# Top-k attention and a gated projection on one core: the last weight piece of a slot goes to GpSimd, and the first pair of slots splits earlier

## The chip, the cores and the metric

One core of a Trainium2 chip. The metric is the time of one execution in microseconds (us), measured on the device. PE is TensorE, DVE VectorE, ACT ScalarE, POOL GpSimd and SP SyncE; SPq is SP's queue, which issues nearly all transfers.

## The reference

```python
def _attn_ref(q, k, v):                       # each 8 x 8 x 576 x 64
    scores = scale * np.matmul(q, k.transpose(0, 1, 3, 2))
    kth = np.partition(scores, -32, axis=-1)[..., -32:-31]
    scores = np.where(scores >= kth, scores, -1e9)
    attn = np.exp(scores - np.max(scores, axis=-1, keepdims=True))
    attn = attn / (np.sum(attn, axis=-1, keepdims=True) + 1e-09)
    return np.matmul(attn, v)

def _moe_ref(x, w_in, w_out):                 # x: 4608 x 512, made of the 8 heads
    h = x @ w_in                              # 512 x 2048
    g = h * (1.0 / (1.0 + np.exp(-1.702 * h)))
    return g @ w_out                          # 2048 x 512
```

`q`, `k` and `v` are 32-bit floats. The two weights come out of the set-up as 64-bit floats, so the kernel reads them as pairs of 32-bit words.

## The kernel before, in words

**Slots.** A batch has 8 heads in 4 pairs, and 576 queries: four tiles of 128 and a tail of 64. A slot is one pair of heads with one tile of queries (or the tails of two pairs), 128 queries of two heads at a time; 18 slots a batch, 144 in all. The order of all instructions is written out by hand: `opening()`, then `slot(n)` for n = 0 to 10 (`SETTLED`), `first_pair(11)`, then pairs of slots in `filling_pair` (from n = 13, `STEADY`) and `steady_pair`, and at the end what is left of the second product.

**A slot's way.** `scores` (PE, sixteen matmuls into four banks), `copy_scores` (ScalarE), `pair_up` (VectorE: larger and smaller of the two halves of the keys, which makes the first two rounds of the search half as wide), `topk` (VectorE: four rounds that find eight values each, three that remove them; 14 operations), `bounds` (GpSimd: the thirty-second and the largest value, scaled), `mask` and `exps` (ScalarE; `exps` sums as well), `invert` (VectorE; from slot 12 on its first half on GpSimd), and then two ways. In slots up to 9, `divide` makes two diagonal matrices of the inverse sums on GpSimd (`by`, a single buffer) and PE multiplies with them to turn the probabilities (`turn_main`, `turn_ends`), and ScalarE copies them out. From slot 10 on, `normalize` (GpSimd) scales the probabilities, `split` (ScalarE) sorts their half-words and SP's queue writes them to memory as `rows`, and `turn_by_dma` reads them back transposed. Last come `values` (PE) and the copy into `xT`. When the four pairs of a tile are done, `hidden` (first product, four chunks of 128 at a time), `tanh` (ScalarE), `gate` (VectorE or GpSimd) and `project` (second product) follow; the first two blocks are done whole, the later ones by seven products of quarters in place of eight. `leave` copies a finished block out on ScalarE; with `project(True)` that waits until `leave_all()`.

**Weights.** There are 32 pieces of 128x512 numbers: two for slot 0 and three each for slots 1 to 10 (`by_slot`). A piece is read into one of seven buffers (`raws`), in the slot before its own, as soon as the piece that lay there is finished, and made into a 32-bit float in five steps: `size` (ScalarE: magnitude of the high word, rebased), `shift` (VectorE: three bits up, which drops the sign bit), `low` (ScalarE: top bits of the low word), `put_sign` (GpSimd: the sign, as a 16-bit zero, into the upper half of the low word) and `add` (GpSimd). `slot(n)` does the sizes after the copy of the scores, the shifts behind the thirteenth of the search's 14 operations, the lows at the end, and the signs and additions in slot n + 1: three of these six before the diagonals, three behind them.

**Queues.** Each engine works in order. In slots 4 to 10, GpSimd's is: bounds, sign, addition, sign, two diagonals, addition, sign, addition. ScalarE's is: mask, exponentials, copy of the scores, tanh, three sizes, copies out of PE's turns, three lows (in slot 5 the tanh comes behind the lows).

**The opening.** `prepare_first` turns the first pair of heads, `scores(0)` and `pair_first` follow, then PE turns the second pair (`prepare`, of which `prepare_ends` is the tails), and `scores(1)`. `stay_warm(count)` is a number of matmuls whose result nobody reads.

**The first pair.** `first_pair(11)` handles slots 11 and 12: `find(m, at)` runs a search and puts `pair_up` behind its eighth operation and `invert(m - 1)` behind operation `at`.

Of the kernel before, what the change touches and what calls it, by code (L numbers as in the profile page):

```python
# [33 lines left out]
def kernel(  # L34
# [101 lines left out]
    def round_piece(n):  # L136

        c, g = pieces[n]
        dst = wout[:, g, :] if c is None else win[:, c, g * PIECE : (g + 1) * PIECE]
        both = raw.pop(n)  # L140
        words = both.rearrange("p (n w) -> p n w", w=2)
        low, high = words[:, :, 0], words[:, :, 1].bitcast(F32)
        parts = both.bitcast(U16).rearrange("p (n h) -> p n h", h=4)
        sign = parts[:, :, 1].bitcast(F16)
        bits, whole = dst.bitcast(U32), dst.bitcast(I32)

        def put_sign():
            nc.gpsimd.tensor_scalar(sign, high, TO_ZERO, 1.0, op0=ALU.mult, op1=ALU.mult)

        def add():  # L150
            nc.gpsimd.tensor_tensor(out=whole, in0=whole, in1=low.bitcast(I32), op=ALU.add)
            finished.append(None)

        return {
            "size": lambda: nc.scalar.activation(dst, high, AF.Abs, scale=REBASE),
            "shift": lambda: nc.vector.tensor_scalar(bits, bits, 3, None, op0=ALU.logical_shift_left),
            "low": lambda: nc.scalar.mul(out=low.bitcast(I32), in_=low, mul=2.0**-29),
            "finish": [put_sign, add],
        }
# [87 lines left out]
    def prepare(name, b, hp):  # L247
        prepare_main(name, b, hp)
        if name == "k":
            prepare_ends(b, hp)  # L250
# [98 lines left out]
    def pair_first():  # L349

        sc = st[0]["sc"] = scp.tile([P, 2, S], F32, name="sc")
        ranked[0] = rank.tile([P, 2, 2, HALF], F32, name="ranked")
        part = lambda i, c: (sc[:, i, c * HALF : (c + 1) * HALF], score_banks[:, i, c, 0:HALF])
        for i in range(2):
            nc.scalar.copy(out=part(i, 1)[0], in_=part(i, 1)[1])
            for c, op in enumerate((ALU.max, ALU.min)):
                nc.vector.tensor_tensor(out=ranked[0][:, i, c, :], in0=part(i, 0)[1], in1=part(i, 1)[0], op=op)
        for i in range(2):
            nc.scalar.copy(out=part(i, 0)[0], in_=part(i, 0)[1])

    def topk(n):

# [67 lines left out]
    def divide(n):  # L430

        invert(n)
        by = st[n]["by"] = diagonals[:]
        for i in range(2):
            nc.gpsimd.tensor_scalar(by[:, i, :], ident[:], st[n]["rden"][:, i : i + 1], 1.0, op0=ALU.mult, op1=ALU.mult)
# [412 lines left out]
    def finish_one():  # L848
        unfinished.pop(0)()
# [34 lines left out]
    def opening():  # L884

        stay_warm(8, v_tail[:, 0, :, :].rearrange("p j d -> p (j d)"))
        load("q", 0, 0, nc.sync)
        load("k", 0, 0, nc.scalar)
        for hp in range(2):
            for name in "qk":  # L890
                if hp:
                    load(name, 0, hp)
        for x in by_slot[0]:
            load_piece(x)
        prepare_first()
        scores(0)
        pair_first()
        stay_warm(2)
        for name in "qk":
            prepare(name, 0, 1)  # L900
        early.extend(round_piece(x) for x in by_slot[0])
        for piece in early:
            piece["size"]()
        scores(1)
        copy_scores(1)
        prepare_rest()
        for hp in range(2, NP):
            for name in "qk":
                load(name, 0, hp)
        load_v(0, 0)  # L910
        for x in by_slot[1]:
            load_piece(x)
# [11 lines left out]
    def slot(n):  # L924

        todo = later.pop(n, [])
        for fn, args in todo:
            if fn not in (prepare, prepare_by_dma, load_piece):
                fn(*args)
        preparing = [(fn, args) for fn, args in todo if fn is prepare or fn is prepare_by_dma]  # L930
        some = [round_piece(x) for x in by_slot.get(n, [])] if n else early
        steps = {name: [piece[name] for piece in some] for name in ("size", "shift", "low")}

        def do(name, count):
            for _ in range(min(count, len(steps[name]))):
                steps[name].pop(0)()

        if n == 0:
            steps["size"].clear()
            do("low", 3)  # L940
        else:
            exponentials(n - 1, bring_all if n % 4 == 1 and n > TURNS + 1 else lambda: None)
            if n == TURNS + 1:
                stay_warm(14)
                bring_all()
            copy_scores(n + 1)
            bring_all()
            if 1 < n <= TURNS:
                turn_main(n - 2)
                turn_ends(n - 2)  # L950
            if n > TURNS + 1:
                tanh(False)
            do("size", 3)
            if n == TURNS + 1:
                do("low", 3)
                tanh(False)
        for i, op in enumerate(topk(n)):
            op()
            if i == 1:
                for _ in range(min(3, len(unfinished))):  # L960
                    finish_one()
            if i == (9 if n < 3 else 7):
                if n > 0:
                    divide(n - 1)
                while unfinished:
                    finish_one()
                for fn, args in todo:
                    if fn is load_piece:
                        fn(*args)
            if i == 9:  # L970
                pair_up(n + 1)
            if i == 12:
                do("shift", 3)
            if i == (13 if n == TURNS + 1 else 10):
                gate()
        bounds(n)
        for piece in some:
            unfinished.extend(piece["finish"])
        if n < NP:
            for fn, args in preparing:  # L980
                fn(*args)
        if n >= TURNS:
            turn_main(n - 1)
            turn_ends(n - 1)
        do("low", 3)
        scores(n + 2)
        if n == SETTLED:
            copy_scores(n + 2)
        if n == 0:
            return  # L990
        idle = not ready and n < TURNS
        if 1 < n <= TURNS:
            values(n - 2, put_off if n == TURNS else None)
        if n >= TURNS:
            values(n - 1, put_off)
        if n >= NP:
            for fn, args in preparing:
                fn(*args)
        if n > PROJECTS and may_project(2):
            project(n == SETTLED)  # L1000
        if idle:
            stay_warm(8)
        hidden()
# [23 lines left out]
    def find(m, at):  # L1027

        for i, op in enumerate(topk(m) if live(m) else [lambda: None] * 14):
            op()  # L1030
            if i == 7 and live(m) and live(m + 1):
                pair_up(m + 1)
            if i == at and live(m - 1):
                invert(m - 1)
            if i > 1 and len(unfinished) > (2 if m == SETTLED + 1 else 0):
                finish_one()
# [5 lines left out]
    def first_pair(n):  # L1042

        begin, prepare_some = dues(n)
        gate()
        bring_all()
        exponentials(n - 1)
        find(n, 10)
        scores(n + 2)
        copy_scores(n + 2)  # L1050
        leave_all()
        tanh(True)
        prepare_some()
        some = [round_piece(x) for x in by_slot.get(n, [])]
        for piece in some:
            piece["size"]()
        hidden(ps_t)
        project_one()
        normalize(n - 1)
        tanh(True)  # L1060
        bounds(n)
        finish_one()
        finish_one()
        for piece in some:
            piece["shift"]()
            piece["low"]()
            unfinished.extend(piece["finish"])
        while unfinished:
            finish_one()
        split(n - 1)  # L1070
        begin(0)
        turn_by_dma(n - 1)
        exponentials(n, leave_all)
        find(n + 1, 10)
        project_one()
        scores(n + 3)
        copy_scores(n + 3)
        leave_all()
        normalize(n)
        split(n)  # L1080
        begin(1)
        turn_by_dma(n)
        bounds(n + 1)
        gate()
        summing.extend(weight_sums("t1", "b12", "b11") + weight_sums("t2", "b22", "t1") + weight_sums("t4", "b21", "t2"))
# [176 lines left out]
```

## Time and profile before

| | |
|---|---|
| median of 3 runs | 1389.51 us (1389.18 to 1391.13) |
| the profiled execution | 1392.55 us, of which its span 1390.8 us |
| TensorE clock granted over the span | 0.987 |
| PE, VectorE, ScalarE, GpSimd busy | 97%, 93%, 83%, 70% |
| PE busy from 0 to 200 us, in stretches of 20 us | 16.0, 11.3, 15.9, 17.9, 17.2, 17.2, 17.8, 18.8, 15.3, 18.2 |
| slots 1 to 10 | from 23 to 140 us |
| slots 11 and 12, the first pair | from 140 to 162 us |

A row of a timeline gives the start, the time, the engine, the line, the operation, what it writes and reads, the count of operations that follow one another, and in brackets how long the engine had been idle and what released it. Several operations in one row overlap a little. A row of a group gives the count, the busy time and the mean of one in ns.

### The profile page before, as it was taken

The numbers are of one execution on the slowest core, as the hardware profiler recorded it, in microseconds if no ns is written. First come the engines' busy times: TensorE is split into PE (matmuls) and PEld (weight loads), VectorE is DVE, ScalarE is ACT, GpSimd is POOL, SyncE is SP. The second block draws the span as 40 slices with busy tenths as digits, with TensorE's granted clock in tenths as the row PEclk, the third lists the DMA queues.
The fourth block names the chain that finished last, engine by engine and source line by source line (L and its number), as shares of the span: only waits on it lengthen the run. The fifth ranks groups of instructions, "written<-read, shape, count | busy, mean of one in ns | idle before, by whom it ended". The sixth has DMA issues, their size and how long they took to land.

```text
span 1390.8 us, 54385 instructions
## 1 busy us (share of the span) xinstructions
PE 1345.4 (97%) x22544; PEld 1207.2 (87%) x22544; DVE 1289.9 (93%) x3394; ACT 1158.5 (83%) x1932; POOL 969.5 (70%) x1758
## 2 busy tenths in 40 slices
PE   6798899999999999999999999999999999999998
PEld 5686578899999998999999999999999999999997
DVE  6999889999999999999999999999999999999912
ACT  5787778999999997999999998899998998888831
POOL 2777686677777776777777777777776777777770
PEclk8899999999999999999999999999999999999999
DMA  7452455977798677977898779888898867755640
GB/s 230 139 153 84 110 149 151 218 193 198 195 225 205 181 179 183 223 193 194 200 206 214 202 177 192 195 197 196 192 218 214 191 181 181 175 142 138 155 115 17
DMA packets 527223, 246.92 MB, mean 178 GB/s; under 512 B 458880, under 2 KB 505472, under 8 KB 526976
## 3 DMA queue, kind: packets, MB, share of 16 engines
q1 hardware_dynamic: 526544, 243.16, 71.4%
q8 instruction: 177, 2.90, 0.9%
q14 instruction: 70, 0.57, 0.1%
q10 hardware_dynamic: 432, 0.30, 0.1%
HBM read 46.01 MB, written 103.42 MB: 107 GB/s over the span
## 4 chain that ended last, share of the span: by engine, by line
PE 87%; POOL 3%; DMA 3%; DVE 3%; ACT 3%; issue 1%; SPq 0%; DVEq 0%; POOLq 0%; ACTq 0%
PE ph L644 33%; PE po L750 29%; PE s_ps L326 11%; PE o L573 10%; DMA pt<-rows 2%; PE po L644 2%; PE po L735 1%; DVE top L373 1%; ACT sc L477 1%; PE tp L455 1%; DVE ranked L377 1%; PE o L513 1%; PE po L172 1%; PE o L544 0%; DMA rows<-sc 0%
## 5 line engine op out<-in xcount | busy, mean ns | idle before, releaser
L373 DVE MAX8 top<-ranked 128x8 f32<-128x288 f32 (+1 forms) x1152 | 637.3, 595 | 0.0
L644 PEld LDWEIGHTS ph<-xT,win 128*64 128x64 f32 (+1 forms) x8736 | 479.7, 137 | 29.0 <-issue 25.4
L644 PE MATMUL ph<-xT,win 128*64 128x128 f32 (+1 forms) x8736 | 504.5, 273 | 0.0
L377 DVE MATCH_REPLACE8 ranked<-top,ranked 128x288 f32<-128x288 f32 (+1 forms) x864 | 462.3, 542 | 0.0
L477 ACT COPY sc<-pr 128x2304 uint16<-128x2304 uint16 x134 | 283.5, 2116 | 93.0 <-POOL pr L441 93.0
L441 POOL TENSOR_SCALAR pr<-pr,rden 128x576 f32<-128x576 f32 x268 | 197.4, 746 | 51.4 <-DVE rden L428 51.1
L415 ACT ACTIVATE pr<-sc,low 128x576 f32<-128x576 f32 x288 | 220.0, 770 | 0.0
L405 ACT ACTIVATE sc<-sc,cut 128x576 f32<-128x576 f32 x288 | 208.9, 780 | 9.1 <-POOL cut L391 9.0
L750 PE MATMUL po<-raws,h 128*64 128x128 f32 x2112 | 205.2, 273 | 0.8 <-POOL h L698 0.8
L750 PE MATMUL po<-wout,h 128*64 128x128 f32 x2112 | 205.2, 273 | 0.1
L347 DVE TENSOR_TENSOR ranked<-s_ps,sc 128x576 f32<-128x576 f32 x286 | 201.8, 747 | 2.8 <-ACT sc L337 2.8
L337 ACT COPY sc<-s_ps 128x576 f32<-128x576 f32 x286 | 168.4, 642 | 26.1 <-PE s_ps L326 19.9
L424 POOL TENSOR_SCALAR some<-den 128x2 f32<-128x2 f32 x132 | 29.1, 220 | 225.7 <-ACT pr L415 225.5
L326 PE MATMUL s_ps<-qk_t 64*64 64x288 f32 x2304 | 177.5, 422 | 3.9 <-DVE ranked L347 3.7
L673 POOL TENSOR_TENSOR th<-th,h 128x512 f32<-128x512 f32 x134 | 171.4, 1279 | 11.2
L750 PE MATMUL po<-wout,th 128*64 128x128 f32 x2176 | 165.2, 273 | 0.1
L750 PEld LDWEIGHTS po<-raws,h 128*64 128x64 f32 x2112 | 133.4, 137 | 1.0 <-POOL h L698 1.0
L750 PEld LDWEIGHTS po<-wout,h 128*64 128x64 f32 x2112 | 133.4, 137 | 0.6 <-POOL h L699 0.6
L750 PEld LDWEIGHTS po<-wout,th 128*64 128x64 f32 x2176 | 127.7, 137 | 1.0 <-POOL th L673 0.6
L326 PEld LDWEIGHTS s_ps<-qk_t 64*64 64x64 f32 x2304 | 76.2, 134 | 57.6 <-issue 13.7
L573 PE MATMUL o<-pt,v_l 128*64 128x128 f32 (+1 forms) x2240 | 124.8, 265 | 0.0
L573 PEld LDWEIGHTS o<-pt,v_l 128*64 128x64 f32 x2240 | 110.3, 137 | 10.1 <-issue 9.5
(108 smaller groups left out, 1633.4 us busy)
## 6 DMA issues: line engine op xcount, KB each, us to landing
rows<-sc SPq DMA_DIRECT2D x134, 576.0 KB, 3.8
qk_rows<-halves SPq DMA_DIRECT2D x24, 576.0 KB, 5.5
out_dram<-raws SPq DMA_DIRECT2D x68, 128.0 KB, 3.7
raws<-in_moe_w_in_dram SPq DMA_DIRECT2D x16, 512.0 KB, 5.0
raws<-in_moe_w_out_dram SPq DMA_DIRECT2D x16, 512.0 KB, 3.5
qk_l<-in_q_dram SPq DMA_DIRECT2D x28, 256.0 KB, 4.4
qk_l<-in_k_dram SPq DMA_DIRECT2D x28, 256.0 KB, 4.6
v_l<-in_v_dram SPq DMA_DIRECT2D x4, 1024.0 KB, 7.9
```

Of the source, the lines that this page charges most:

```text
L326: nc.tensor.matmul(ps[rows, i, c, 0:HALF], lhsT=qT[b, hps[p]][on, cols], rhs=kT[b, hps[p]][on, FIRST[i] + c * HALF : FIRST[i] + (c + 1) * ...
L347: nc.vector.tensor_tensor(out=ranked[n][:, :, c, :], in0=a, in1=b, op=op)
L373: nc.vector.max(top[:, i, 8 * r : 8 * r + 8], of(r, i))
L377: nc.vector.match_replace(to, top[:, i, 8 * r : 8 * r + 8], of(r, i), LOWEST)
L405: nc.scalar.activation(sc[:, i, :], sc[:, i, :], AF.Prelu, bias=cut[:, i : i + 1], scale=SCALE, alpha=HUGE)
L415: nc.scalar.activation(pr[:, i * S : (i + 1) * S], sc[:, i, :], AF.Exp, bias=low[:, i : i + 1], accum_out=den[:, i : i + 1],)
L441: nc.gpsimd.tensor_scalar(pr[:, i, :], pr[:, i, :], st[n]["rden"][:, i : i + 1], 1.0, op0=ALU.mult, op1=ALU.mult)
L477: nc.scalar.copy(out=halves, in_=pr[:].bitcast(U16).rearrange("p (k h) -> p h k", h=2))
L573: nc.tensor.matmul(o[s][j * D : (j + 1) * D, cols], lhsT=lhsT, rhs=rhs, start=(s, j) not in halves[:k], stop=(s, j) not in halves[k + 1 :],)
L644: nc.tensor.matmul(ph[rows, i * P : (i + 1) * P], lhsT=win[:, c, f * P + rows.start : f * P + rows.stop], rhs=xs[:, x.place, c, :], start= ...
L673: nc.gpsimd.tensor_tensor(out=th[:], in0=th[:], in1=h, op=ALU.mult)
L750: nc.tensor.matmul(both_banks[y * TAIL : (y + 1) * TAIL, bank, to * P : (to + 1) * P], lhsT=a[:, i, :], rhs=weight(w, fs[i])[:, y, :], sta ...
```

## The change

- **Opening.** `pair_first` works on both heads at a time: one copy of 128x576 and two VectorE operations of 128x576 in place of two copies and four operations of 128x288, and one copy at the end in place of two. Between the turns of the second pair's main tiles and of its tails stand eight more matmuls of `stay_warm`.
- **Weights.** In slots with three pieces the last piece's magnitude is made on GpSimd (`pool_size`: a multiplication that keeps the sign bit, which `shift` drops) and its sign on ScalarE (`sign`, behind the lows). From slot 3 on `pool_size` stands behind the third of GpSimd's sign and addition steps and ahead of the diagonals; in slots 1 and 2 behind the diagonals.
- **First pair.** `invert` comes behind the ninth operation of both searches in place of the eleventh; `normalize`, `split`, `turn_by_dma` and `bounds` of the first search come directly behind it, ahead of the next scores and their copy; the additions of the last pieces come ahead of `project_one`; one `project_one`, one `leave_all` and a loop over the pieces of slot 11 (there are none) go.

```diff
+            "pool_size": lambda: nc.gpsimd.tensor_scalar(dst, high, REBASE, 1.0, op0=ALU.mult, op1=ALU.mult),
+            "sign": lambda: nc.scalar.mul(out=sign, in_=high, mul=TO_ZERO),
...
-        part = lambda i, c: (sc[:, i, c * HALF : (c + 1) * HALF], score_banks[:, i, c, 0:HALF])
-        for i in range(2):
-            nc.scalar.copy(out=part(i, 1)[0], in_=part(i, 1)[1])
-            for c, op in enumerate((ALU.max, ALU.min)):
-                nc.vector.tensor_tensor(out=ranked[0][:, i, c, :], in0=part(i, 0)[1], in1=part(i, 1)[0], op=op)
-        for i in range(2):
-            nc.scalar.copy(out=part(i, 0)[0], in_=part(i, 0)[1])
+        half = lambda c: sc[:, :, c * HALF : (c + 1) * HALF]
+        nc.scalar.copy(out=half(1), in_=score_banks[:, :, 1, 0:HALF])
+        for c, op in enumerate((ALU.max, ALU.min)):
+            nc.vector.tensor_tensor(
+                out=ranked[0][:, :, c, :], in0=score_banks[:, :, 0, 0:HALF], in1=half(1), op=op
+            )
+        nc.scalar.copy(out=half(0), in_=score_banks[:, :, 0, 0:HALF])
...
         for name in "qk":
-            prepare(name, 0, 1)
+            prepare_main(name, 0, 1)
+        stay_warm(8)
+        prepare_ends(0, 1)
...
+        last = some[-1] if len(some) > 2 else None
+        if last:
+            steps["size"].pop()
...
             if i == 1:
                 for _ in range(min(3, len(unfinished))):
                     finish_one()
+                if last and n > 2:
+                    last["pool_size"]()
             if i == (9 if n < 3 else 7):
                 if n > 0:
                     divide(n - 1)
+                if last and n < 3:
+                    last["pool_size"]()
...
         for piece in some:
-            unfinished.extend(piece["finish"])
+            unfinished.extend(piece["finish"][piece is last :])
...
         do("low", 3)
+        if last:
+            last["sign"]()
...
         exponentials(n - 1)
-        find(n, 10)
+        find(n, 8)
+        normalize(n - 1)
+        split(n - 1)
+        begin(0)
+        turn_by_dma(n - 1)
+        bounds(n)
+        while unfinished:
+            finish_one()
         scores(n + 2)
         copy_scores(n + 2)
         leave_all()
         tanh(True)
         prepare_some()
-        some = [round_piece(x) for x in by_slot.get(n, [])]
-        for piece in some:
-            piece["size"]()
         hidden(ps_t)
         project_one()
-        normalize(n - 1)
         tanh(True)
-        bounds(n)
-        finish_one()
-        finish_one()
-        for piece in some:
-            piece["shift"]()
-            piece["low"]()
-            unfinished.extend(piece["finish"])
-        while unfinished:
-            finish_one()
-        split(n - 1)
-        begin(0)
-        turn_by_dma(n - 1)
         exponentials(n, leave_all)
-        find(n + 1, 10)
-        project_one()
+        find(n + 1, 8)
         scores(n + 3)
         copy_scores(n + 3)
-        leave_all()
```

## The prediction

> **What bounds the kernel now.** I read the page first, then the busy time in stretches, then the chain that ended last over the first 300 us, and then each engine's timeline up to 260 us, where the change lies.
>
> ```profile
> PE 1345.4 (97%) x22544; PEld 1207.2 (87%) x22544; DVE 1289.9 (93%) x3394; ACT 1158.5 (83%) x1932; POOL 969.5 (70%) x1758
> ...
> PE   6798899999999999999999999999999999999998
> ```
>
> ```profile
> 40.00:60.00 20.00, 15.87 (x140) 12.79 (x140) 19.57 (x48) 14.74 (x31) 15.69 (x17) 0.83 0.47 147
> ...
> 260.00:280.00 20.00, 20.00 (x356) 18.50 (x354) 20.00 (x53) 17.08 (x31) 12.37 (x24) 1.00 1.00 235
> ```
>
> The columns of the second view are the stretch, its length, and the busy time of PE, weight loads, VectorE, ScalarE and GpSimd. From about 260 us PE has no gap left (20.00 of 20), so what the start wins or loses goes through to the end one for one. In the start VectorE sets the pace (19.57 of 20 in slots 2 to 4) and PE waits; from slot 8 on the end hangs on PE. So I follow one path: VectorE from the opening to slot 7, GpSimd's diagonals in slot 8, PE and ScalarE in slots 9 and 10, then the first pair. Figures are shifts on this path; minus is earlier.
>
> **The opening.**
>
> ```profile
> 9.01 1.20 PE L326 MATMUL s_ps<-qk_t 64*64 64x288 f32 x16
> ...
> 10.28 0.40 ACT L355 COPY sc<-s_ps 128x288 f32<-128x288 f32 x1 [2.56 <-PE s_ps L326]
> ...
> 12.73 0.81 DVE L373 MAX8 top<-ranked 128x8 f32<-128x288 f32 x2
> ...
> 14.09 0.48 PE L235 MATMUL tp<-ident,qk_l 128*128 128x128 f32 x1 [2.37 <-ACT qk_t L232]
> 14.58 2.60 PE L326 MATMUL s_ps<-qk_t 64*64 64x288 f32 x16
> 14.92 1.26 ACT L155 ACTIVATE win<-raws 128x512 f32<-128x512 f32 x2
> 17.24 1.18 ACT L337 COPY sc<-s_ps 128x576 f32<-128x576 f32 x2 [1.05 <-PE s_ps L326]
> 18.45 1.42 DVE L347 TENSOR_TENSOR ranked<-s_ps,sc 128x576 f32<-128x576 f32 x2 [1.16 <-ACT sc L337]
> ```
>
> Before, the first pairing runs from 10.28 to 12.73. After, one wide copy (half of the 1.18 of two such: 0.6) and two wide operations (1.42) give 10.28 + 0.6 + 1.4 = 12.3: -0.4, for VectorE and for ScalarE's queue behind it.
>
> The eight idle matmuls go into PE's wait of 2.37, so they cost nothing. Before, PE comes out of that wait at half speed: sixteen score matmuls take 2.60, where the same sixteen took 1.20 at 9.01. With half the gap filled and 0.4 less of it I expect 1.20. Then scores(1) ends at about 15.4, ScalarE's two magnitudes at 15.8 (16.2 before) and its copy at 17.0 (18.4 before). VectorE, free at 18.45 - 1.16 - 0.4 = 16.9, pairs up slot 1 at 17.05: **-1.4**. If PE stays slow, scores(1) ends at 16.8 and -0.4 is left.
>
> **The price of the new GpSimd operation.** No row shows it: 128x512, 32-bit to 32-bit, source at every second word, destination dense. The groups of GpSimd's instructions by shape (count, busy us, mean ns) have its neighbours.
>
> ```profile
> L673 POOL TENSOR_TENSOR th<-th,h 128x512 f32<-128x512 f32 x134 | 171.4, 1279 | 11.2
> L672 POOL TENSOR_SCALAR th<-th 128x512 f32<-128x512 f32 x134 | 82.8, 618 | 0.5 <-ACT th L660 0.5
> ...
> L148 POOL TENSOR_SCALAR raws<-raws 128x512 f16<-128x512 f32 x32 | 43.1, 1347 | 2.8
> ...
> L151 POOL TENSOR_TENSOR win<-win,raws 128x512 int32<-128x512 int32 x16 | 20.9, 1303 | 0.8
> ```
>
> The ends are 0.62 (L672, all dense) and 1.35 (L148, the sign that it replaces: same source, but a 16-bit destination at every fourth half-word). L151 reads one operand at every second word and takes 1.30, the dense L673 1.28: the stride of the source costs next to nothing, so it is L148's destination that is slow, and I take 0.65, with the gap behind it 0.73. Both ends stay in the range. The Trainium skill ("GPSIMD Engine Reference", Performance pitfalls for Q7 kernels) makes reads with a step above 8 bytes half again dearer; a step of 8, as here, would escape it, and the sum would be the same; no run here shows the operation alone. On ScalarE the sign costs what a magnitude does (1.26 for two: some 0.63) and takes one's place, behind the slot's low parts instead of ahead of the copies out of PE's turns.
>
> **Slots 1 to 7.** One line's instructions (shortest, median and longest ns), then rows of the timelines of VectorE, GpSimd, PE and ScalarE:
>
> ```profile
> L156 DVE TENSOR_SCALAR win<-win x16: 406/418/1509, 21.9 to 78.8; 128x512 uint32<-128x512 uint32 x16
> ```
>
> ```profile
> 53.46 2.53 DVE L156 TENSOR_SCALAR win<-win 128x512 uint32<-128x512 uint32 x3
> ...
> 62.34 0.73 POOL L435 TENSOR_SCALAR by<-ident,rden 128x128 f32<-128x128 f32 x2 [0.86 <-PE tp L458]
> 62.77 3.79 PE L455 MATMUL tp<-by,pr 128*128 128x128 f32 x16 [0.52 <-POOL by L435]
> ...
> 67.42 1.80 ACT L157 ACTIVATE raws<-raws 128x512 int32<-128x512 uint32 x3
> ...
> 69.11 1.43 ACT L405 ACTIVATE sc<-sc,cut 128x576 f32<-128x576 f32 x2
> ...
> 71.99 1.34 POOL L148 TENSOR_SCALAR raws<-raws 128x512 f16<-128x512 f32 x1
> ...
> 72.08 1.27 DVE L426 TENSOR_SCALAR some<-den 128x2 f32<-128x2 f32 x1 [0.47 <-ACT pr L415]
> ...
> 101.25 1.72 DVE L156 TENSOR_SCALAR wout<-wout 128x512 uint32<-128x512 uint32 x3
> ```
>
> VectorE's shifts take 0.41 each but up to 1.51 where a GpSimd operation is under way: three unhindered need 1.05, those at 53.46 took 2.53, and the tiny one at 72.08 ended (73.35) just when GpSimd's sign did (73.33). With the last piece's sign gone from behind the diagonals, GpSimd's last addition ends 0.6 to 0.7 sooner against the shifts: in slot 3 it then ends some 0.65 after they start, so -0.85 (1.7 for 2.53), and in slot 2 about -0.3. VectorE leaves slot 3 at -1.4 - 0.3 - 0.85 = **-2.55**.
>
> Slot 4: the magnitude (0.73) stands ahead of the diagonals, which waited 0.86 for PE there, so it is hidden, and PE's turn starts at -2.55. ScalarE copies it out and does the low parts as before; then the sign (+0.65) lies ahead of the mask, which waited for nothing at 69.11: mask, exponentials and sums come at -1.9. VectorE wants those sums in slot 5 and now waits for them longer than the 0.47 before. The tiny operation then falls behind the magnitude instead of the sign: 69.75 + 0.05 + 0.65 + 0.17 = 70.6 for 73.35, **-2.75**. Shifts without hindrance in slot 5 give another -0.3; in slot 6 ScalarE's -1.9 takes back 0.1; in slot 7 the shifts at 101.25 find GpSimd nearly done (1.05 for 1.72): **-3.6** at the bounds that end slot 7.
>
> **Slots 8 to 10.**
>
> ```profile
> 97.61 2.05 PE L455 MATMUL tp<-by,pr 128*128 128x128 f32 x16 [1.74 <-POOL by L435]
> ...
> 108.54 0.73 POOL L435 TENSOR_SCALAR by<-ident,rden 128x128 f32<-128x128 f32 x2
> 108.97 3.52 PE L455 MATMUL tp<-by,pr 128*128 128x128 f32 x16 [2.79 <-POOL by L435]
> ...
> 125.43 0.44 PE L458 MATMUL tp<-by,pr 128*64 128x128 f32 x4 [1.10 <-ACT pt L463]
> ...
> 138.30 0.44 PE L458 MATMUL tp<-by,pr 128*64 128x128 f32 x4 [1.07 <-ACT pt L463]
> ```
>
> In slot 8 the diagonals follow GpSimd's own queue without a gap, so the magnitude delays them by its 0.73, and PE's turn starts at -3.6 + 0.7 = **-2.9**. It took 3.52 after 2.79 of idling; after 1.74 the same turn took 2.05. I keep it slow; at full speed there would be another -1.5. In slots 9 and 10 PE waits 1.1 for copies that stand behind three magnitudes; two leave -0.55 each: **-4.0**. The diagonals are in time there (PE is busy).
>
> **The first pair.**
>
> ```profile
> 154.21 2.12 ACT L477 COPY sc<-pr 128x2304 uint16<-128x2304 uint16 x1
> ...
> 159.22 0.17 DVE L426 TENSOR_SCALAR some<-den 128x2 f32<-128x2 f32 x1 [4.00 <-ACT pr L415]
> ...
> 170.25 0.64 PE L231 MATMUL tp<-ident,raws 128*128 128x128 f32 x4 [0.94 <-DMA raws<-in_k_dram]
> ...
> 185.89 0.23 POOL L424 TENSOR_SCALAR some<-den 128x2 f32<-128x2 f32 x1 [0.63 <-ACT pr L415]
> ```
>
> No piece is left in this slot, so the loop that goes was empty; PE's order stays, as the one projection that is ready runs behind the same hidden product. The split (2.0) leaves the path into a wait of ScalarE; its write and its transpose go ahead of the output's transfers on SP's queue, and the loads that PE waited for at 170.25 come about 1.0 sooner. The copy of the output now lies between mask and exponentials and waits for the projection; the sums come only 0.4 sooner. VectorE asks for them two operations earlier (0.66 + 0.72), which now follow the stall of 4.00: +1.4 - 0.4 = +1.0 for everything behind it on VectorE. GpSimd had 0.63 to spare at 185.89, so **+0.3**. If the loads decide instead, it is -0.9.
>
> **The sum:** -1.4 - 0.3 - 0.85 - 0.2 (lock, less the sign) - 0.3 + 0.1 - 0.65 + 0.7 - 1.1 + 0.3 = -3.7. The profiled execution took 1392.55 (its span 1390.8 and 1.75 around it), 3.0 over the median of 1389.51; the shift is the same for both, so 1389.51 - 3.7 = **1385.8**.
>
> **The rivals.**
>
> *The magnitude is as slow as the sign it replaces* (1.35, 1.42 with its gap). The locks give -0.15 by slot 3; in slot 4 the diagonals come 0.55 behind their old wait; with the sign PE and ScalarE leave 1.3 of 1.55, and VectorE's bounds end slot 7 at -0.7. In slot 8 +1.4 makes +0.7, then -1.1 and +0.3: -0.1, or -1.6 if the longer idling before slot 7's turn (1.74 + 1.6) spares slot 8's. About 1388.5. For it speaks that L148 is the nearest row by engine, shape and source; L151 against L673 speaks against it.
>
> *The idle matmuls don't keep PE fast* at 14.6: 1.0 less all along, 1386.8. For it: 0.75 of the gap remains.
>
> *The magnitude waits for its load.* Its piece was read last, by ScalarE's third magnitude, and is now read some 5 us earlier, in GpSimd's order: diagonals, additions and the next bounds queue behind it, and the ring of seven buffers hands the delay on to the next loads. The rows are SP's queue and the DMA issues up to 60 us (count, KB, median us to landing).
>
> ```profile
> 30.46 10.80 SPq L134 DMA_DIRECT2D raws<-in_moe_w_in_dram  x3
> ```
>
> ```profile
> raws<-in_moe_w_in_dram SPq DMA_DIRECT2D x15, 512.0 KB, 5.1
> ```
>
> Slot 3's last piece is issued at about 41 and lands after a median 5.1, some 1 us ahead of its new reading; in slots 4 and 5 I work out 2.8 and 2.9 to spare. If landings take over 8, three slots wait about 2.2 each: -3.7 + 6.6 = +2.9, 1392.4, slower. Against it: before, GpSimd and ScalarE never waited for a piece.
>
> *The longer idling of PE* bears on all cases. The Trainium skill ("TensorE: Matmul & The Clock Gate", Why this matters for your kernels) warns of gaps over some 3 us, after which the clock halves; here 2.79 was enough, and by that rule the gap of 4.6 that I work out ahead of scores(15), 167 us, costs 1.4 there, beside a path that has about 0.9 to spare: +0.5.
>
> **How the numbers follow.** Forecast 0.52, its own range 1383.0 (slot 8's turn fast, the loads deciding) to 1387; slow magnitude 0.20; slow matmuls 0.13; late loads 0.15. A measurement of this kernel can tell about 0.2%, 2.8 us. Faster than 1386.7: nine tenths of the forecast, half of the slow matmuls, a little of the slow magnitude: 0.56. Slower than 1392.3: the late loads and a little, 0.16. The rest 0.28. The range of 1382.8 to 1390.2 leaves out the late loads and the outermost of the rest.
>
> **What would show it.** Right: GpSimd's new operation near 0.65; sixteen score matmuls at about 14.2 in 1.2; slot 1's pairing at 17.05; the three shifts of slot 3 in about 1.7; PE's slot 8 turn about 2.9 earlier; waits of 0.55 where 1.1 stood; VectorE's stall in the first pair at about 5 instead of 4. Wrong: the new operation over 1 us, GpSimd waiting for a load in slots 1 to 5, ScalarE waiting for GpSimd's bounds later than before, or PE idling for longer in slots 7 and 8 than it did.

## The result, and the profile after

| | before | after |
|---|---|---|
| median of 13 runs each | 1390.18 us (1387.40 to 1394.16) | 1386.68 us (1383.92 to 1390.91) |
| ratio, 95% interval | | 0.9974 [0.9963, 0.9986] |
| the profiled execution, and its span | 1392.55, 1390.8 | 1387.0, 1385.2 |

The kernel is 3.5 us faster; 3.7 was predicted. First the page of the kernel after (busy time of the engines; PE's busy tenths in 40 slices) and its busy time in the same two stretches.

```profile
PE 1345.7 (97%) x22560; PEld 1209.1 (87%) x22560; DVE 1283.0 (93%) x3392; ACT 1165.2 (84%) x1930; POOL 963.8 (70%) x1758
...
PE   7889889999999999999999999999999999999998
```

```profile
40.00:60.00 20.00, 15.56 (x128) 12.91 (x125) 19.53 (x54) 17.07 (x34) 15.73 (x21) 0.84 0.55 172
...
260.00:280.00 20.00, 20.00 (x358) 18.07 (x352) 20.00 (x55) 19.33 (x31) 13.96 (x28) 1.00 0.92 182
```

The picture is the old one: VectorE full in the first slots, PE without a gap from 260 to 280 us. Over the whole kernel VectorE is busy for 6.9 us less, GpSimd for 5.7 less, ScalarE for 6.7 more. Where each comes from, the groups of instructions up to 150 us show (count, busy us, mean ns; what follows the second bar is the idle time ahead). Kernel after, GpSimd and ScalarE:

```profile
L156 POOL TENSOR_SCALAR wout<-raws 128x512 f32<-128x512 f32 x6 | 4.0, 658 | 0.5
L156 POOL TENSOR_SCALAR win<-raws 128x512 f32<-128x512 f32 x4 | 2.7, 668 | 1.2 <-DMA raws<-in_moe_w_in_dram 1.1
...
L148 POOL TENSOR_SCALAR raws<-raws 128x512 f16<-128x512 f32 x22 | 29.7, 1350 | 1.9
```

```profile
L157 ACT ACTIVATE raws<-raws 128x512 f16<-128x512 f32 x10 | 13.6, 1364 | 0.3
L155 ACT ACTIVATE win<-raws 128x512 f32<-128x512 f32 x12 | 7.5, 681 | 0.0
```

The magnitude (`wout<-raws` and `win<-raws` on L156, and L155 on ScalarE) costs 0.66 on GpSimd, as priced. The sign on ScalarE (L157) costs 1.36, not the 0.63 at which it was priced: twice the magnitude that it replaces there (0.68).

VectorE's shifts and its tiny operation ahead of the reciprocal, up to 150 us, before and then after:

```profile
L156 DVE TENSOR_SCALAR win<-win 128x512 uint32<-128x512 uint32 x16 | 10.5, 708 | 0.0
L156 DVE TENSOR_SCALAR wout<-wout 128x512 uint32<-128x512 uint32 x16 | 7.0, 489 | 0.0
L426 DVE TENSOR_SCALAR some<-den 128x2 f32<-128x2 f32 x11 | 6.6, 604 | 2.3 <-ACT pr L415 2.3
```

```profile
L158 DVE TENSOR_SCALAR win<-win 128x512 uint32<-128x512 uint32 x16 | 7.5, 519 | 0.0
L158 DVE TENSOR_SCALAR wout<-wout 128x512 uint32<-128x512 uint32 x16 | 5.8, 414 | 0.0
L428 DVE TENSOR_SCALAR some<-den 128x2 f32<-128x2 f32 x11 | 4.6, 421 | 6.5 <-ACT pr L417 6.5
```

The same 43 instructions take 17.9 in place of 24.1. These 6.2 are time in which VectorE stood still inside an instruction, since the work is the same. Against that stand 4.2 more of waiting for ScalarE's sums (6.5 for 2.3).

**Where the time went.** To compare two profiles I count from the first copy of scores in the opening (ScalarE; 10.28 before, 8.87 after), since nothing of the change lies ahead of it. Timelines of the kernel after (VectorE, GpSimd, PE):

```profile
15.39 1.42 DVE L349 TENSOR_TENSOR ranked<-s_ps,sc 128x576 f32<-128x576 f32 x2
...
39.21 1.85 DVE L158 TENSOR_SCALAR win<-win 128x512 uint32<-128x512 uint32 x3
...
50.12 1.40 DVE L158 TENSOR_SCALAR win<-win 128x512 uint32<-128x512 uint32 x3
...
68.34 0.17 DVE L428 TENSOR_SCALAR some<-den 128x2 f32<-128x2 f32 x1 [2.60 <-ACT pr L417]
...
103.21 0.38 DVE L428 TENSOR_SCALAR some<-den 128x2 f32<-128x2 f32 x1 [2.10 <-ACT pr L417]
```

```profile
98.06 0.22 POOL L393 TENSOR_SCALAR cut<-top 128x4 f32<-128x4 f32 x1 [2.05 <-DVE top L375]
...
103.95 0.73 POOL L437 TENSOR_SCALAR by<-ident,rden 128x128 f32<-128x128 f32 x2 [0.40 <-DVE rden L430]
...
179.28 0.23 POOL L426 TENSOR_SCALAR some<-den 128x2 f32<-128x2 f32 x1
```

```profile
12.66 1.45 PE L328 MATMUL s_ps<-qk_t 64*64 64x288 f32 x16 [0.16 <-ACT qk_t L234]
...
93.21 3.39 PE L457 MATMUL tp<-by,pr 128*128 128x128 f32 x16 [3.48 <-POOL by L437]
104.38 2.05 PE L457 MATMUL tp<-by,pr 128*128 128x128 f32 x16 [1.27 <-POOL by L437]
...
131.22 0.44 PE L460 MATMUL tp<-by,pr 128*64 128x128 f32 x4 [0.30 <-ACT pt L465]
...
160.16 2.20 PE L328 MATMUL s_ps<-qk_t 64*64 64x288 f32 x16 [5.00 <-DVE ranked L349]
...
188.85 0.48 PE L237 MATMUL o<-ident,qk_l 128*128 128x128 f32 x1 [2.66 <-ACT qk_t L234]
...
195.59 0.66 PE L646 MATMUL ph<-xT,win 128*64 128x128 f32 x8
...
255.77 3.66 PE L646 MATMUL ph<-xT,win 128*64 128x128 f32 x64
```

| counted from the first copy of scores | before | after | shift | predicted |
|---|---|---|---|---|
| slot 1's first pairing (VectorE) | 8.17 | 6.52 | -1.65 | -1.4 |
| end of slot 3's shifts | 45.71 | 42.65 | -3.06 | -2.55 |
| end of slot 5's tiny operation | 63.07 | 59.64 | -3.43 | -2.75 |
| bounds that end slot 7 | 93.45 | 89.19 | -4.26 | -3.6 |
| start of PE's turn in slot 8 | 98.69 | 95.51 | -3.18 | -2.9 |
| PE's last turn of slot 10 | 128.02 | 122.35 | -5.67 | -4.0 |
| slot 14's sums taken up by GpSimd | 175.61 | 170.41 | -5.20 | -3.7 |
| a block of 64 first-product matmuls, PE (260.23 before) | 249.95 | 246.90 | -3.05 | -3.7 |

From the last of these starts to the end of the span it is 1130.6 before and 1129.4 after. In the eleven kernels below this rest is 1128.3 to 1133.8 with the same instructions: PE still waits in it, for between 0.15 and 3.2 us in all, mostly for the probabilities that come back transposed from memory (`pt<-rows`; 1.8 in all before, 0.4 after, 3.2 with the magnitude alone). So single profiles place a gain within the first 250 us, and only the ratios say what it is worth at the end.

The gain was 5.2 at slot 14 and 3.05 at 250 us. In between lies the wait of 2.66 at 188.85: it was 1.31 before, and behind it PE's clock is halved. The busy time in stretches of about 3.4 us, kernel after (the last three figures are the granted clock, the DMA share and GB/s):

```profile
185.00:188.20 3.20, 1.20 (x9) 0.89 (x8) 3.20 (x9) 3.20 (x7) 3.20 (x5) 1.00 0.91 275
188.20:191.60 3.40, 2.75 (x22) 2.42 (x24) 0.78 (x3) 1.09 (x4) 3.02 (x4) 0.50 0.03 5
191.60:195.00 3.40, 3.40 (x36) 2.60 (x36) 3.40 (x9) 0.94 (x7) 1.37 (x4) 0.50 0.51 116
```

Two whole stretches run at 0.50, and the first product behind them starts 6.74 after the row at 188.85 (195.59) where 3.83 pass without the halving (third experiment: 195.90 to 199.73): 2.9 given back.

### The profile page after: what moved, and what is told of

The parts are those of the page before. It is cut to its first block, busy times and chain, and to the rows that moved or that the text cites. A ratio compares the mean times of both kernels' runs of the same rounds, so it can differ in the third digit from the quotient of the medians.

```text
span 1385.2 us, 54404 instructions
## 1 busy us (share of the span) xinstructions
PE 1345.7 (97%) x22560; PEld 1209.1 (87%) x22560; DVE 1283.0 (93%) x3392; ACT 1165.2 (84%) x1930; POOL 963.8 (70%) x1758
```

## The experiments

Each is an edit of the changed kernel or of the one before. The ratio is to the kernel before, run on the same chip, with its 95% interval; the last three columns count from the first copy of scores in its own profile.

| | ratio | median, and before's | slot 1's pairing | bounds ending slot 7 | last turn of slot 10 |
|---|---|---|---|---|---|
| before | 1 | | 8.17 | 93.45 | 128.02 |
| after | 0.9974 [0.9963, 0.9986] | 1386.68, 1390.18 | 6.52 | 89.19 | 122.35 |
| opening alone | 0.9999 [0.9990, 1.0007] | 1389.98, 1390.76 | 6.52 | 91.80 | 126.32 |
| weights alone | 0.9975 [0.9964, 0.9985] | 1387.01, 1390.76 | 7.03 | 89.11 | 122.58 |
| first pair alone | 0.9995 [0.9983, 1.0006] | 1390.18, 1390.76 | 8.17 | 93.38 | 127.91 |
| opening and weights | 0.9971 [0.9959, 0.9983] | 1385.83, 1390.76 | 6.52 | 87.96 | 122.01 |
| weights, sign only | 0.9972 [0.9961, 0.9983] | 1386.64, 1390.09 | 7.30 | 88.02 | 121.62 |
| weights, magnitude only | 0.9999 [0.9989, 1.0010] | 1390.09, 1390.09 | 7.02 | 92.86 | 125.38 |
| after, magnitude made twice | 1.0005 [0.9996, 1.0014] | 1390.63, 1390.09 | 6.52 | 91.19 | 125.99 |
| after, PE kept busy at 188 us | 0.9962 [0.9950, 0.9974] | 1385.20, 1390.09 | 6.52 | 88.51 | 121.84 |
| opening and sign | 0.9971 [0.9959, 0.9984] | 1385.92, 1390.85 | 6.52 | 86.96 | 121.37 |
| the same, PE kept busy | 0.9971 [0.9959, 0.9984] | 1387.35, 1390.85 | 6.52 | 87.00 | 121.34 |
| after, without the 8 idle matmuls | 0.9972 [0.9962, 0.9982] | 1387.48, 1390.85 | 6.52 | 88.00 | 121.73 |

**The three parts, each alone.** The opening alone, the weights alone and the first pair alone are the kernel before with the hunks of that part; the fourth is the changed kernel with the first pair as it was:

```diff
-        find(n, 8)
-        normalize(n - 1)
-        split(n - 1)
...
+        find(n, 10)
...
-        find(n + 1, 8)
+        find(n + 1, 10)
```

> The kernel before with the opening alone (the wide first pairing and the eight idle matmuls). All points are measured from the start of the first copy of scores on ScalarE, which takes out the phase of the clock at the start. Theory (the steps of the prediction): slot 1 is paired up at about 6.5 us after that copy (8.17 before, 6.52 after), VectorE hands the whole 1.65 down to the bounds that end slot 7 (93.45 before, about 91.8 expected), and the kernel gains 1 to 2 us. Rival: ScalarE's late mask in slot 5, which hangs on PE's half-speed turn, takes the gain back, and the bounds that end slot 7 stand within 0.4 of before; the total is the same within 0.5.

> The kernel before with the moved weight steps alone (the last piece's magnitude on GpSimd, its sign on ScalarE). Theory: the new GpSimd operation takes 0.66; slot 1 is paired up at 8.17 after the first copy as before; the bounds that end slot 7 come about 2.6 earlier than before (93.45 to about 90.8), the last turn of slot 10 about 4 earlier (128.0 to about 124), and the kernel gains 2 to 4. Rival (the magnitude is paid for by the diagonals and by the loads it waits for): GpSimd waits over 1 us for loads in slots 1 to 5, PE's turn in slot 8 comes no earlier than before, and the gain stays under 1.

> The kernel before with the new first pair alone. Theory: nothing changes up to the last turn of slot 10 (128.0 after the first copy). VectorE's stall in the pair grows from 4.0 to about 5, so the sums of slot 14 on GpSimd come 0.3 to 0.6 later (175.6 to about 176.0), while PE's own chain, freed of its wait for the output's copy, comes about 1 earlier; the wait of PE for ScalarE's copy ahead of the tails of queries and keys then grows from 1.31 to over 2, the clock halves there, and the hidden product that starts at 189.0 comes 2 to 3 later. The kernel loses 1 to 3. Rival: the loads decide, everything behind the pair comes 0.9 earlier, and the kernel gains about 1.

> The changed kernel with the first pair of before, so the opening and the weight steps together. Theory: the last turn of slot 10 at about 122.4 after the first copy, as in the changed kernel; behind it the old first pair hands on the whole 5.7, without the long wait ahead of the tails (1.3, not 2.7), so that the hidden product that stood at 189.0 starts near 183.5, and the kernel beats the changed one by 1 to 3. Rival: the new first pair is a gain of its own, and this kernel is 1 slower than the changed one.

The weights alone give what the whole change gives. The opening alone is within 0.1% of nothing, though its profile has slot 1's pairing 1.65 earlier, as the changed kernel's: -1.65 is left at the bounds that end slot 7 and -1.70 at slot 10, and the interval (-1.4 to +1.0 us) does not bear out so much at the end. Both the weights alone and the sign alone (further down) have the old opening. PE's timeline in the one, then in the other:

```profile
13.20 0.33 PE L237 MATMUL tp<-ident,qk_l 128*128 128x128 f32 x1 [2.37 <-ACT qk_t L234]
13.69 1.45 PE L328 MATMUL s_ps<-qk_t 64*64 64x288 f32 x16 [0.16 <-ACT qk_t L234]
```

```profile
12.77 0.33 PE L237 MATMUL tp<-ident,qk_l 128*128 128x128 f32 x1 [2.37 <-ACT qk_t L234]
13.25 1.73 PE L328 MATMUL s_ps<-qk_t 64*64 64x288 f32 x16 [0.16 <-ACT qk_t L234]
```

The same instructions after the same wait of 2.37 took 2.60 in the kernel before, here 1.45 and 1.73. So 1.1 of the 1.65 is a slow clock that the old opening meets in some executions: its pairing comes at 8.17, 8.17, 7.30, 7.03 and 7.02 in five profiles, the new one's at 6.52 in all eight. Against an old opening at full speed the new one saves 0.5.

Opening and weights with the old first pair were expected to beat the changed kernel by 1 to 3; 0.9971 against 0.9974 doesn't show it. The first pair alone moves the time by nothing that can be told (by its interval -2.4 to +0.8 us). Its cost was seen: GpSimd takes slot 14's sums 48.06 behind slot 10's last turn, 47.59 before, +0.47, and 48.06 in the changed kernel too. PE's wait ahead of the turns of the tails grows as in the changed kernel, but here no slow stretch follows (the first product 3.83 behind, as above):

```profile
195.90 0.33 PE L235 MATMUL o<-ident,qk_l 128*128 128x128 f32 x1 [2.55 <-ACT qk_t L232]
...
199.73 0.44 PE L644 MATMUL ph<-xT,win 128*64 128x128 f32 x4
```

**Sign or magnitude.** The weights alone, but in the one all three magnitudes stay on ScalarE, in the other all three signs stay on GpSimd:

```diff
-        if last:
-            steps["size"].pop()
...
-                if last and n > 2:
-                    last["pool_size"]()
...
-                if last and n < 3:
-                    last["pool_size"]()
```

```diff
-            unfinished.extend(piece["finish"][piece is last :])
+            unfinished.extend(piece["finish"])
...
-        if last:
-            last["sign"]()
```

> The kernel before, with only the last piece's sign moved from GpSimd to ScalarE; its magnitude stays on ScalarE. Times from the first copy of scores in the opening, against 93.45 (bounds that end slot 7) and 128.0 (last part of slot 10's turn) of before. Theory (half of the gain is the lock: GpSimd's 1.35 sign goes from where VectorE's shifts find it): the shifts take near 1.1 in all slots, the bounds of slot 7 come about 2.5 earlier, and nothing is added in slots 9 and 10, where ScalarE still has three magnitudes ahead of the copies and PE still waits 1.1: the last turn about 2.5 earlier, the kernel 1.5 to 2.5 faster. Rival (the gain is ScalarE's missing magnitude): the sign only adds to ScalarE's queue, and the kernel is the same or up to 1 slower.

> The kernel before, with only the last piece's magnitude moved from ScalarE to GpSimd; its sign stays on GpSimd. Theory: GpSimd's queue grows by 0.7 a slot, the shifts are held up as before or longer, the bounds of slot 7 come between 0 and 1 later than 93.45, the diagonals of slot 8 0.7 later still, and PE's waits in slots 9 and 10 fall from 1.1 to 0.5: in sum between 0.5 faster and 1 slower. Rival (the gain is ScalarE's missing magnitude): 2 to 4 faster, like both together.

As far as the ratios can tell, all of the gain belongs to the sign: 0.9972 without the new magnitude, 0.9999 with the magnitude alone. VectorE's groups up to 150 us, sign only and then magnitude only:

```profile
L158 DVE TENSOR_SCALAR win<-win 128x512 uint32<-128x512 uint32 x16 | 6.3, 445 | 0.0
L428 DVE TENSOR_SCALAR some<-den 128x2 f32<-128x2 f32 x11 | 6.0, 549 | 3.2 <-ACT pr L417 3.2
L158 DVE TENSOR_SCALAR wout<-wout 128x512 uint32<-128x512 uint32 x16 | 5.8, 416 | 0.0
```

```profile
L158 DVE TENSOR_SCALAR win<-win 128x512 uint32<-128x512 uint32 x16 | 12.7, 846 | 0.0
L158 DVE TENSOR_SCALAR wout<-wout 128x512 uint32<-128x512 uint32 x16 | 6.3, 443 | 0.0
L428 DVE TENSOR_SCALAR some<-den 128x2 f32<-128x2 f32 x11 | 4.6, 423 | 2.3 <-ACT pr L417 2.3
```

Together 18.1 with the sign gone and 23.6 with the magnitude added, against 24.1 before: what GpSimd does at the moment of the shifts is what VectorE pays. That GpSimd's own queue is merely shorter doesn't explain it: in the kernel before, GpSimd waited 1.38 to 2.14 for VectorE ahead of the bounds that end slots 3 to 7, so these could come earlier only through VectorE. The Trainium skill ("SBUF — State Buffer", SBUF: two separate sides) calls the port pair that VectorE and GpSimd share an exclusive lock, held for the whole instruction. The trace agrees: with the magnitude alone a shift that takes 406 ns unhindered took 846 in the mean and up to 1519, and before, the tiny operation at 72.08 ended just when GpSimd's sign did.

The magnitude does shorten PE's waits for ScalarE's copies in slots 9 and 10, as predicted: 0.53 and 0.52 in place of 1.10 and 1.07 (sign only: 1.03 and 1.07). PE with the magnitude alone:

```profile
123.31 0.44 PE L460 MATMUL tp<-by,pr 128*64 128x128 f32 x4 [0.53 <-ACT pt L465]
...
135.63 0.44 PE L460 MATMUL tp<-by,pr 128*64 128x128 f32 x4 [0.52 <-ACT pt L465]
```

It pays 0.56 back between slot 1's pairing and slot 7's bounds (85.84 for 85.28) and 0.65 from there to PE's turn in slot 8 (5.89 for 5.24). In the time nothing of it is left to see (by its interval -1.5 to +1.4 us).

**The magnitude made twice** doubles its cost on GpSimd; in slots 1 and 2, where it stands behind the diagonals, likewise:

```diff
                 if last and n > 2:
                     last["pool_size"]()
+                    last["pool_size"]()
...
```

> The changed kernel with GpSimd's magnitude done twice (0.66 becomes 1.33, the price of the sign it stands in for). Theory: the lock and the diagonals take the 0.67 in slots 7 and 8 and part of it in slots 2 to 5; the bounds of slot 7 come about 2 later than the 89.2 of the changed kernel, the turn of slot 8 another 0.7, and the kernel gives back 1.5 to 2.5 of its 3.6 (ratio to before 0.9985 to 0.999). Rival: the second one is hidden in GpSimd's waits, and the ratio stays near 0.9974.

Ten more of 0.66 turn 0.9974 into 1.0005: some 4.3 us (each ratio is known to about 1.5) for 6.6 of GpSimd's time. By slot 7's bounds 2.0 of it is lost, at slot 10 3.6. So most of the time added at this place of GpSimd's queue reaches the end.

**PE kept busy at 188 us.** Sixteen matmuls that nobody reads (the profile records each as two), in the wait ahead of the turns of the tails:

```diff
         second_part.clear()
+        if n == STEADY + 2:
+            for _ in range(16):
+                nc.tensor.matmul(both_banks[:, 0, 0:P], lhsT=ident[:], rhs=ident[:], start=True, stop=True)
```

> The changed kernel with sixteen matmuls more that nobody reads, in PE's wait of 2.66 for ScalarE's copy ahead of the tails of queries and keys (slot 15), where its profiled execution then ran at half speed for 6.8 us. Theory: they take about 2 of the wait and no time; the clock stays at full speed there in every execution, the hidden product behind starts 3.7 after the tails as in the other kernels (6.7 in the changed one), and the median gains 0.5 to 2.5 on the changed kernel, by how often that wait halves the clock. Rival: GpSimd's loop sets the end there, and the ratio stays near 0.9974.

The slow stretch is gone from the profile, and the ratio is the lowest of all; but the intervals of 0.9962 and 0.9974 overlap, so a gain isn't shown.

**What is left of the change at its cheapest:** the opening and the sign, with ScalarE's magnitudes and the first pair as before; the same with the sixteen matmuls; and the changed kernel without the opening's eight:

```diff
         for name in "qk":
             prepare_main(name, 0, 1)
-        stay_warm(8)
         prepare_ends(0, 1)
```

> The changed kernel with all three magnitudes back on ScalarE and with the first pair as it was before: of the change only the opening and the sign on ScalarE are left. If the sign alone makes the gain and the opening's earlier start (-1.65 at the first pairing of slot 1) goes on through slots 1 to 10, the turn of slot 10 comes about 120.5 us behind the first copy of scores (121.62 with the sign alone, 122.35 in the changed kernel) and the ratio to before is 0.996 to 0.997. Rival: the magnitude on GpSimd is worth its 0.55 in each of slots 9 and 10; then slot 10's turn is no earlier than the 122.0 of opening and weights together, and the ratio is 0.9975 to 0.998.

> As the kernel with the sign and the opening alone, with sixteen matmuls that nobody reads in PE's wait ahead of the turns of the tails at about 188 us, where the clock was halved in the changed kernel's profile. If that halving is a matter of chance that costs 2.2 to 2.9 in some executions, this takes it away: the same turn in slot 10, hidden products from 183 to 185 in place of 186.7, and a ratio 0 to 0.002 below that of the kernel without them, about 0.9955 and below both kernels of the case. Rival: PE has no time for them there when the sums come early, or the clock did not halve there anyway; then the ratio is equal or up to 0.001 higher (sixteen matmuls of about 0.1 us).

> The changed kernel without the eight idle matmuls of the opening. The prediction's rival: without them PE comes out of its wait of about 2 us at half speed, the sixteen matmuls of scores(1) take 2.6 in place of 1.45, slot 1's first pairing comes 1.0 to 1.2 later (7.6 against 6.5 behind the first copy of scores), and the time is about 1 higher than the changed kernel's, ratio 0.998. Theory from the other profiles: half speed falls on some stretches whatever this one wait is, so the matmuls have little to do with it: pairing at 6.5 to 7.0 in an execution without a half-speed stretch there, and a ratio of 0.9974 as in the changed kernel.

The opening and the sign have the earliest profile so far (86.96 at slot 7, and 121.37 at slot 10, where 120.5 was expected), and 0.9971, as good as the changed kernel. The rival had slot 10's turn no earlier than 122.0 and a ratio of 0.9975 to 0.998: the profile speaks against it, the interval of the ratio doesn't exclude it. In the second of these kernels slot 14's sums came 0.85 later than in the first, and the sixteen matmuls took 3.74, more than the wait that they were to fill (1.22 without them). So the tails start at 191.16 in place of 188.38, and nothing is won:

```profile
187.59 3.74 PE L1134 MATMUL po<-ident 128*128 128x128 f32 x32
191.16 0.27 PE L237 MATMUL o<-ident,qk_l 128*128 128x128 f32 x1
```

Without the eight idle matmuls, PE's timeline has a wait of 1.86 and still full speed behind it, and pairing and ratio are unchanged. So this execution doesn't bear out that half speed follows when they are left out:

```profile
13.37 0.33 PE L237 MATMUL tp<-ident,qk_l 128*128 128x128 f32 x1 [1.86 <-ACT qk_t L234]
13.86 1.45 PE L328 MATMUL s_ps<-qk_t 64*64 64x288 f32 x16 [0.16 <-ACT qk_t L234]
```

That is one execution. The last section shows, from all thirteen profiles, that the eight do spare others the slow clock; in the time no difference is seen. No version here is shown to beat the changed kernel; the sign alone, a few lines, equals it as far as the ratios can tell.

## Why the prediction was right, point by point

The total came out (-3.5 for -3.7), and the main mechanism, the sign gone from the way of VectorE's shifts, is shown by the pair of sign and magnitude. That the total is so close is partly luck: by the medians the weights were worth about 0.9 more than the sum had and the opening less, and the two made up for each other.

- **Opening, -1.4.** Seen in the profile as -1.65 (the sixteen matmuls in 1.45, not 1.20, and the copies earlier than reckoned), but 1.1 of it is a clock that was slow in the execution profiled. The three pairs of kernels that differ by the opening (alone against before, with the weights, with the sign) differ by 0.0001, 0.0004 and 0.0001: 0.1 to 0.6 us, each known to some 1.5. So the term was probably too large, by about 1. The mechanism, that the idle matmuls keep PE fast, holds for the clock in every profile (last section), but PE is often fast without them as well. Its rival, that they don't keep PE fast, falls.
- **Price of the magnitude, 0.65:** 0.66. The rival at 1.35 falls. Had it held, the doubled magnitude says that nothing of the gain would have been left, where the rival reckoned with 1388.5.
- **Price of the sign on ScalarE, 0.63:** the step that failed, 1.36. In slot 5, where it lies ahead of the mask, VectorE's wait for the sums became 2.60 in place of 0.47; some 0.7 of that is the mistake in the price. The tiny operation there, which the prediction puts behind GpSimd's magnitude from a time of 69.75 that no row gives, ran unhindered behind that wait (0.17).
- **Locks.** Larger than reckoned: slot 2's shifts 2.49 to 1.85 (-0.64 for -0.3), slot 3's 2.53 to 1.40 (-1.13 for -0.85), slot 4's 2.77 to 1.36, slot 7's in 1.08 as forecast. The weights alone are worth -3.5 [-5.0, -2.1] in the time; the sum without opening and first pair had -2.6.
- **Slot 8's diagonals, +0.7:** +1.08 between bounds and turn, for another reason: behind the magnitude they still wait 0.40 for VectorE's reciprocal, ahead of which VectorE waited 2.10 for ScalarE's sums. Ahead of slot 7's turn PE idled for 3.48 (1.74 before) and the turn ran slow (3.39 for 2.05), ScalarE's copies behind it were late, and slot 8's turn ran at full speed, 2.05 for 3.52. That is the -1.5 that the prediction named and did not take.
- **Slots 9 and 10, -0.55 each:** the waits of 1.10 and 1.07 became 0.06 and 0.30 in the changed kernel, with 0.20 of waiting for the diagonals new, and 0.53 and 0.52 with the magnitude alone. In both, slot 10's last turn starts 24.65 behind slot 8's, 25.89 before: -1.24 for -1.1.
- **First pair, +0.3:** +0.47. PE idled 5.00 ahead of scores(15) (4.6 reckoned) and took 2.20 there. VectorE's stall did not become 5; it was 3.61 in the changed kernel and 3.97 in the first pair alone.
- **Late loads.** In the changed kernel GpSimd waited for a load once, 1.08 in slot 1 (the group's 1.1 above), behind the diagonals, and 0.2 to 0.4 there in four of the experiments; the prediction had reckoned with slots 3 to 5. The rival falls.
- **The slower clock** as a case for all: right that longer waits are paid for so, but not where. The profile's largest give-back (2.9) came at 188 us, where nothing had been reckoned.
- **One for one from 260 us on:** not borne out by single profiles, whose rest varies by 5.5 us. The profile of the magnitude alone starts the block of 64 matmuls 3.1 earlier than before (246.86 for 249.95), and its median time equals that before. Whether earlier arrival itself makes the later waits longer stays open.
- **The signs of being wrong:** two were seen, GpSimd's wait for a load in slot 1 and PE's longer idling ahead of slot 7's turn. Neither turned the total. Of the signs of being right, VectorE's stall of 5 did not come.

## What to carry to other kernels

Price an instruction by what it writes as well as by what it reads: the sign, a 16-bit result into every fourth half-word, costs 1.35 on GpSimd and 1.36 on ScalarE, twice the 0.66 and 0.68 of a dense 32-bit result from the same source. Whether the width or the step of the result makes it slow, no run here separates. On GpSimd look for work that lies under VectorE's instructions, as VectorE's rows show it by durations far above their shortest. Taking one such operation a slot away gave all of the gain that can be told, while ten more of another cost about two thirds of their own time. And before a stretch of PE is read as won or lost, see whether its clock was halved in that execution.

## What was not expected of the hardware

PE's granted clock changes on a fixed grid, and the same wait is followed by a slow stretch or not. In all thirteen traces the record of the clock consists of stretches of 3.41 us and whole multiples of it; the slow ones last 3.41, 6.83 or, at 24 us in the last three kernels, 10.24. The kernel before in the opening, then the weights alone, cut about where their own records are:

```profile
10.30:13.70 3.40, 1.42 (x12) 1.19 (x12) 2.53 (x8) 1.62 (x5) 0.00 (x0) 1.00 1.12 318
13.70:17.10 3.40, 3.00 (x17) 1.37 (x17) 3.40 (x11) 2.40 (x7) 0.00 (x0) 0.50 0.83 181
17.10:20.50 3.40, 3.40 (x23) 2.71 (x20) 2.24 (x5) 2.98 (x6) 0.00 (x0) 0.50 0.77 195
```

```profile
11.86:15.27 3.41, 1.91 (x21) 1.08 (x23) 3.41 (x14) 3.29 (x10) 0.00 (x0) 1.00 0.85 180
15.27:18.68 3.41, 2.19 (x21) 1.41 (x17) 3.40 (x8) 3.41 (x7) 0.00 (x0) 1.00 0.77 174
```

The wait of 2.37 is the same. In the first, 2.0 of it lie in one stretch of the grid, PE is busy for 1.42 of that stretch, and half speed follows. In the second a mark of the grid cuts it into 1.0 and 1.3, the later stretch still holds 1.91 of work, and full speed follows. This holds throughout: of the full-speed stretches in the first 280 us of the thirteen profiles, the 63 with PE busy for less than 1.45 were all followed by half speed and the 813 with more than 2.04 all by full speed; of the 41 between, 13 by half speed. So it is not the length of a wait that decides, but how it falls on the grid. At the tails of queries and keys a wait of 2.66 left 1.40 of a stretch busy (kernel after) and one of 2.09 left 1.33 (magnitude twice), and both were followed by half speed; 2.55 was cut by a mark into 3.05 and 1.89 (first pair alone), and full speed followed. In the six profiles without the eight idle matmuls the stretch around the opening's wait held 1.25, 1.36, 1.42, 1.45, 1.65 and 1.91, and the first three were followed by half speed; with the eight it held at least 3.18 in all seven, and none was.

The Trainium skill ("TensorE: Matmul & The Clock Gate", What's actually happening) has a free-running window of 3413 ns in which activity is watched; the grid agrees with that. That the spread of the times comes from where the grid falls in an execution is argued only, not shown.
